# A long-convolution transform split 32 by 32 instead of 128 by 8, on small tiles of the matrix array

## The chip, the cores and the metric

The kernel runs on one core of one Trainium2 chip. The metric is the device time of one execution in microseconds (us). The engines are PE (TensorE, matmul; its weight loads are listed as PEld), DVE (VectorE), ACT (ScalarE), POOL (GpSimd) and SP (SyncE, which here only issues DMAs). SBUF is the on-chip memory in 128 partitions, PSUM the accumulator memory of PE, in 8 banks of 512 fp32 numbers per partition.

## The reference, cut to what matters

Two kinds of layer alternate on one sequence of S = 2048 tokens with D = 512 channels: a long-convolution mixer A and a channel MLP B, each with a residual and a layer norm in front.

```python
def _A_ref(q, k, v, shift_k, ssm_k, ssm_D):
    k_shift = <causal FIR of 4 taps per channel on k>
    kv = k_shift * v
    y = irfft2(rfft2(pad(kv)) * rfft2(pad(ssm_k)))[:S]     # causal convolution of length S
    y = y + kv * ssm_D
    return q * y
def _B_ref(x, w1, b1, w2, b2):                             # F = 1376
    h = gelu(layernorm(x) @ w1 + b1)
    return h @ w2 + b2
x = A_q
for _ in range(2):
    x = x + _A_ref(layernorm(x), A_k, A_v, ...)
    x = x + _B_ref(layernorm(x), B_x, B_w1, ...)
```

The convolution result y depends on k, v and the filter only, not on x. So it is computed once and used by both layers.

## The kernel before, in words

The sequence is cut into two halves of 1024 tokens. The convolution is done through a transform of length 2048 in bf16, per half: data half 0 with filter half 0 gives the output of half 0; half 1 needs data half 1 with filter half 0 plus data half 0 with filter half 1. The helper functions carry tags, which the text uses:

- `turn` (tags ht0, ht1): PE transposes bring the filter from channels-on-partitions to time-on-partitions (line 536).
- `shift_turn` and `shift`, `shift_pair` (kt, fir): the FIR of 4 taps as matmuls with diagonal weights, in half 0 on 64-row tiles of the array (line 610), in half 1 on 32-row tiles (line 638); DVE multiplies with v (lines 616, 647).
- `stage1` (h1, x1): first step of the transform, 128 matmuls per call in 8 groups, each 128 rows by 64 columns of the array, 128 columns streamed (line 553).
- `stage2` (h2, x2): second step with twiddles in a table `R_S2` of 128 x 16384 bf16 (4 MB, 16 loads of 256 KB): 128 matmuls per call in 8 groups, full array, 64 columns streamed (line 565).
- `swap`: 8 DMAs SBUF to SBUF that exchange even and odd partitions of the filter's spectrum.
- products on DVE (`tt`, line 464), `inverse1` (i1; 128 matmuls per half, line 665) and `inverse2` (i2; 16 matmuls of 512 columns per half, line 683).

Every group ends with an evacuation from PSUM by ACT or DVE (`evac`, lines 469 and 470), of 128 x 1024 numbers in most.

The MLP follows in blocks of 128 or 256 tokens for half 0 and of 512 for half 1: norms (DVE, POOL, ACT), a DMA transpose by SP (line 866; a PE transpose for the first two, line 874), `m1` with w1 (line 886, 44 matmuls a block), gelu on ACT (line 891), `m2` with w2 (line 920, 11 matmuls per 128 tokens), the residual on DVE (line 924) and stores. The last 128 tokens are done in three pieces (lines 909, 913).

What sets the order: the program first records all operations; `SEQ` is a list, fixed in the source, of all operation numbers in the order of issue, `ENGS` says which engine takes each operation that may go to several, and `BANKS` gives each PSUM tile its bank. `arrange` splits SEQ into one in-order queue per engine, and `sync` puts semaphore waits where one queue needs another. DMAs are issued by SP in their place of SEQ, a few by ACT. The convolution of half 1 stands in SEQ between the MLP operations of half 0. A "matmul" in the source is two instructions of PE: a weight load and a multiplication.

## Time and profile before

| | |
|---|---|
| median of 3 runs | 238.55 us (238.39 to 239.25) |
| span of the profiled execution | 238.6 us, from the first to the last instruction (no other time of that execution is given) |
| PE busy | 226.9 us in 2615 matmuls; weight loads 152.3 us |
| DVE, ACT, POOL busy | 178.1, 159.6, 55.3 us |
| first matmul of the MLP (line 886) | 60.40 us after the span's start |
| last DVE operation (line 913) | begins at 236.23 us |
| DMA | 26.75 MB, of it 0.34 MB in 21 packets of the queue named "instruction" |

How to read it: "busy" of PE counts pipelined matmuls, so it is not work at full speed. The time line lists instructions in order of time, merged, with the idle time before them in brackets and who ended it; "issue" there means that the engine waited for nothing that the profile shows. The chain of waits is followed back from the last instruction. A row of windows gives the busy time of each engine in a stretch with the number of its instructions, the granted clock of PE, the mean busy share of the 16 DMA engines and their rate.

### The profile page before, as it was taken

Reading aid. Unit: us, or ns where it says so; the run is one execution under the profiler, and the core shown is the slowest. Engines: PE = TensorE matmul, PEld = TensorE weight load, DVE = VectorE, ACT = ScalarE, POOL = GpSimd, SP = SyncE. Lnnn points to the kernel's source line nnn. Section 1 sums busy time; section 2 is a strip of 40 time slices with the busy share of each in tenths; the row PEclk is TensorE's granted clock in tenths of the full one; section 3 lists DMA queues with packets and bytes.
Section 4 is the critical chain, followed back from the end, with each engine's and each line's share of the span. In section 5 each row is a group of like instructions: output and inputs, shape, how many; then the busy total and the mean of one; then the engine's idle time right before and its main releaser. Section 6 shows DMA issues by size and latency. Waiting matters only on the chain.

```text
span 238.6 us, 6251 instructions
## 1 busy us (share of the span) xinstructions
PE 226.9 (95%) x2615; PEld 152.3 (64%) x2637; DVE 178.1 (75%) x358; ACT 159.6 (67%) x255; POOL 55.3 (23%) x120
## 2 busy tenths in 40 slices
PE   6998698899999999999999999999999999999995
PEld 3897588885968588667769675644445444444454
DVE  0579869999999999999999999593579469404013
ACT  2586879999996899999768786359036606831630
POOL 2421030104623506446004522303020210200000
PEclk9999979999999999999999999999999999999999
DMA  6999767989946660053100304200300050132202
GB/s 173 350 393 388 272 181 186 257 267 194 163 87 197 153 140 3 1 69 103 54 0 15 80 0 83 49 3 12 78 0 3 18 157 0 25 66 91 84 0 91
DMA packets 41112, 26.75 MB, mean 112 GB/s; under 512 B 23702, under 2 KB 33788, under 8 KB 41084
## 3 DMA queue, kind: packets, MB, share of 16 engines
q1 hardware_dynamic: 40786, 26.20, 40.5%
q8 instruction: 21, 0.34, 0.6%
q10 hardware_dynamic: 298, 0.16, 0.3%
q14 instruction: 7, 0.06, 0.1%
HBM read 15.07 MB, written 2.10 MB: 72 GB/s over the span
## 4 chain that ended last, share of the span: by engine, by line
PE 83%; DVE 6%; DMA 4%; ACT 3%; issue 2%; POOL 1%; SPq 1%; POOLq 0%
PE ps L886 32%; PE ps L920 31%; PE ps L665 6%; PE ps L553 5%; PE ps L565 3%; ACT ar L469 3%; DMA ar<-in_A_ssm_k_dram 2%; DVE ar L464 2%; DMA ar<-ar 2%; DVE ar L616 1%; PE ps L683 1%; PE ps L909 1%; PE ps L638 1%; PE ps L610 1%; DVE ar L470 1%
## 5 line engine op out<-in xcount | busy, mean ns | idle before, releaser
L891 ACT ACTIVATE ar<-ps,sm 128x256 bf16<-128x256 f32 (+4 forms) x143 | 65.4, 525 | 41.0 <-PE ps L886 39.5
L469 ACT ACTIVATE ar<-ps 128x1024 bf16<-128x1024 f32 (+3 forms) x77 | 71.3, 1005 | 16.4 <-PE ps L553 6.4
L886 PE MATMUL ps<-ar 128*128 128x256 bf16 (+4 forms) x568 | 81.5, 297 | 0.3
L920 PE MATMUL ps<-ar 128*128 128x512 bf16 (+1 forms) x324 | 77.2, 379 | 1.1 <-issue 0.3
L886 PEld LDWEIGHTS ps<-ar 128*128 128x128 bf16 (+1 forms) x572 | 52.8, 100 | 28.1 <-ACT ar L891 0.4
L464 DVE TENSOR_TENSOR ar<-ar 128x512 bf16<-128x512 bf16 (+3 forms) x105 | 62.7, 637 | 0.9 <-ACT ar L469 0.4
L920 PEld LDWEIGHTS ps<-ar 128*128 128x128 bf16 (+1 forms) x341 | 32.4, 98 | 33.4 <-ACT ar L891 0.2
L924 DVE TENSOR_TENSOR ar<-ar,ps 128x512 bf16<-128x512 bf16 x31 | 20.7, 678 | 33.2 <-PE ps L920 33.0
L797 DVE BATCH_NORM_STATS2 sm<-ar 128x6 f32<-128x512 bf16 x64 | 42.9, 683 | 0.5
L822 ACT ACTIVATE ar<-ar,sm 128x512 bf16<-128x512 bf16 x34 | 26.4, 811 | 9.5 <-DVE sm L809 8.3
L804 POOL TENSOR_TENSOR sm<-sm 128x2 f32<-128x2 f32 (+2 forms) x26 | 23.6, 909 | 23.8 <-DVE sm L802 22.0
L802 POOL TENSOR_SCALAR sm<-sm 128x2 f32<-128x2 f32 (+2 forms) x21 | 6.4, 304 | 97.3 <-DVE sm L798 97.1
L553 PE MATMUL ps<-ar 128*64 128x128 bf16 x512 | 18.6, 227 | 3.1 <-issue 1.4
L565 PEld LDWEIGHTS ps<-ar 128*128 128x128 bf16 x512 | 18.4, 102 | 3.4 <-ACT ar L469 1.0
L565 PE MATMUL ps<-ar 128*128 128x64 bf16 x512 | 19.6, 199 | 0.5 <-ACT ar L469 0.4
L553 PEld LDWEIGHTS ps<-ar 128*64 128x64 bf16 x512 | 15.7, 114 | 6.1 <-issue 2.6
L812 POOL TENSOR_SCALAR sm<-sm 128x1 f32<-128x1 f32 x43 | 16.1, 390 | 2.0
L470 DVE CAST ar<-ps 128x1024 bf16<-128x1024 f32 x11 | 13.3, 1222 | 4.3 <-PE ps L565 2.8
L665 PE MATMUL ps<-ar 128*128 128x128 bf16 x256 | 15.0, 219 | 0.5 <-DVE ar L464 0.4
L665 PEld LDWEIGHTS ps<-ar 128*128 128x128 bf16 x256 | 14.7, 113 | 1.2 <-DVE ar L464 0.6
L823 DVE TENSOR_SCALAR ar<-ar,sm 128x512 bf16<-128x512 bf16 x30 | 11.8, 410 | 3.4 <-POOL sm L812 3.1
L470 DVE COPY ar<-ps 128x1024 bf16<-128x1024 bf16 (+1 forms) x9 | 5.5, 632 | 8.0 <-PE ps L516 5.3
(41 smaller groups left out, 94.3 us busy)
## 6 DMA issues: line engine op xcount, KB each, us to landing
ar<-tab_s SPq DMA_DIRECT2D x16, 256.0 KB, 9.0
ar<-ar SPq DMA_DIRECT2D x16, 256.0 KB, 3.7
ar<-in_A_ssm_k_dram SPq DMA_DIRECT2D x8, 256.0 KB, 6.8
ar<-in_A_q_dram SPq DMA_DIRECT2D x8, 256.0 KB, 4.7
ar<-in_A_v_dram SPq DMA_DIRECT2D x8, 256.0 KB, 6.1
out_dram<-ar SPq DMA_DIRECT2D x7, 256.0 KB, 2.5
ar<-in_B_w_dram SPq DMA_DIRECT2D x4, 344.0 KB, 4.8
ar<-in_B_w_dram SPq DMA_DIRECT2D x5, 256.0 KB, 4.0
```

What stands on the lines that cost most here:

```text
L464: return P.op(eng, lambda e: e.tensor_tensor(o, a, b, op), dur, reads=[a, b] + list(more), writes=[o])
L469: return e.activation(dst, src(), AF.Copy)
L470: return e.tensor_copy(dst, src())
L553: r = e.matmul(Q(tl, 64 * ri, 64, i * 128, [1, 128]), w, m, start=True, stop=True)
L565: r = e.matmul(Q(tl, 0, 128, i // 8 * 512 + i % 8 * 4, [32, 16], [1, 4]), w, m, start=True, stop=True)
L665: r = e.matmul(Q(tl, 0, 128, i * 128, [1, 128]), w, m, start=n == 0, stop=n == 1)
L797: P.op(DVE, lambda e, sj=sj, x=x: e.bn_stats(sj, x), 600.0, reads=[x], writes=[sj])
L804: P.op(POOL, lambda e: e.tensor_tensor(r, v, hf, ALU.pow), 420.0 + 149.0 * n, reads=[v, hf], writes=[r])
L822: return e.activation(o, x, AF.Identity, bias=u, scale=r)
L886: r = e.matmul(Q(tl, 0, rows, 0, [1, w]), a, m, start=dk == 0, stop=dk == 3)
L891: P.op(ACT, lambda e, dst=dst, tl=tl, rows=rows, bias=bias, w=w: e.activation(dst, Q(tl, 0, rows, 0, [1, w]), AF.Gelu_apprx_tanh, bias=bia ...
L920: r = e.matmul(Q(tl, 0, 128, 0, [1, 512]), ins[fc][0], ins[fc][1], start=fc == 0, stop=fc == 10)
```

## The change

The transform's two steps have 32 x 32 points instead of 128 x 8. All tensors of the convolution are laid out anew: a group of 32 partitions holds 32 blocks of time or frequency of 128 channels. The matmuls then have 32 or 64 rows of the array, or 32 or 64 columns of it, and several lie beside each other in the array.

- The table of `stage2` shrinks from 128 x 16384 to 128 x 4096 bf16 (1 MB, 4 loads).
- Matmuls per half (before, then after): turn 32, then 256 in half 0 (`turn0`, two halves of the channels, each once its own two loads are there) and 128 in half 1 (`turn1`); stage1 128 per call, then 128 on 32-row tiles with 64 columns streamed; stage2 128 per call, then 256 on tiles of 32 x 64 with 128 columns streamed; FIR 88 in half 0 and 176 in half 1, then 352 in each on tiles of 64 x 32; inverse1 128, then 256 on 64-row tiles; inverse2 16 of 512 columns, then 256 on tiles of 32 x 32 with 128 columns streamed, in PSUM tiles of 4 banks.
- The evacuations stay 8 per step of 128 x 1024 numbers. The products on DVE keep their sizes, with runs of 16 numbers instead of 64.
- The swap's 8 DMAs move 2048 contiguous numbers per partition; each needs all 8 groups of stage2 (before, each needed four of them).
- v is loaded in 4 DMAs of 32 partitions in runs of 128 numbers (256 bytes), q in 4 DMAs of 32 partitions in runs of 8 KB. Stores are 4 DMAs of 32 partitions where one of 128 stood: 32 in all for 11; some go to ACT's queue.
- 40 warm-up matmuls in 10 groups of 4 are added and stand at places in the new SEQ. The filter half 1 (ht1, h1_1) shares memory with the data of half 0 and stands later. `paced` falls away (it had no effect with its distance of 99).
- SEQ, ENGS and BANKS are new.

```diff
-    S2 = S2.transpose(0, 1, 2, 3, 5, 6, 4).reshape(128, 128 * 128)
+    S2 = S2.reshape(32, 4096)
...
-        for j in range(8):
-            tl = Tile(2)
-            ins = [(ri, i, src(8 * j + i), A(0, 128, R_F + 128 * ri, [1, 128])) for i in range(8) for ri in range(2)]
-                    r = e.matmul(Q(tl, 64 * ri, 64, i * 128, [1, 128]), w, m, start=True, stop=True)
+    def mms(tl, ins, dur):
+        def f(e):
+            for tile, p0, n, off, dims, w, m, a, z in ins:
+                r = e.matmul(Q(tile, p0, n, off, *dims), w, m, start=a, stop=z)
+            return r
+        P.op(PE, f, dur, reads=[x for y in ins for x in y[5:7]], tile=tl)
...
+    def turn0():
+        for i in range(2):
+            tt(o, o, A(64 * i, 64, R_TC + 4, [5, 4]), ALU.add, {DVE: 70.0, POOL: 200.0}, (DVE, POOL))
+            for h in (1, 0):
+                src = [(a, g, A(64 * i, 64, hraw + 1024 * g + 16 * h + a, [32, 32])) for a in range(16) for g in range(4)]
+                        r = e.transpose(QB(tl, 32 * g, 32, a * 64, [1, 64]), s, idn)
...
+    def stage1(x, G):
+        for gp in range(2):
+            for hi in range(4):
+                mms(tl, [(tl, 0, 128, 512 * g + 64 * lo, ([1, 64],), A(64 * gp + 32 * g, 32, x + 1024 * hi + lo, [8, 128]),
+                          A(64 * gp + 32 * g, 32, R_F, [1, 64]), True, True) for lo in range(8) for g in range(2)], 240.0)
...
     def stage2(G, t):
-        ins = [(i, A(0, 128, R_S2 + (16 * t + i) * 128, [1, 128]), A(0, 128, G + (16 * t + i) * 8, [1024, 8], [1, 8])) for i in range(16)]
+        mms(tl, [(tl, 64 * (d // 2), 64, 512 * (d % 2) + 4 * i, ([16, 4], [64, 8], [1, 4]),
+                  A(32 * d, 32, R_S2 + 128 * (4 * t + i) + 64 * ri, [1, 64]), A(32 * d, 32, G + 256 * (4 * t + i) + 128 * ri, [1, 128]), ri == 0, ri == 1)
+                 for i in range(4) for ri in range(2) for d in (0, 2, 1, 3)], 460.0)
...
+    def shift(half):
+        for b in range(4):
+            for a in steps:
+                for r in range(2):
+                    for g in range(4):
+                        k = A(64 * r, 64, R_KT + 1152 * g + a % 8 * 144 + (16 if a >= 0 else 15) + b, [4, 32])
+            mms(tl, ins, 900.0)
...
+    def inverse2(Z, YT, groups):
+        for n in groups:
+            tl = Tile(4)
+            mms(tl, [(tl, 32 * j, 32, 512 * g + 128 * i, ([1, 128],), A(32 * g, 32, R_T2 + 32 * (2 * (8 * j + s0 + i) + ri), [1, 32]),
+                      A(32 * g, 32, Z + 128 * (2 * (8 * j + s0 + i) + ri), [1, 128]), ri == 0, ri == 1)
+                     for i in range(n) for ri in range(2) for j in range(4) for g in range(4)], 230.0 * n)
...
+                    def store(c, n, last=False):
+                        for j in range(4):
+                            src = A(32 * j, 32, R_X[half] + c, [1, n])
+                            outs.append(dma(dr(out, 512 * (1024 * half + 8 * j) + c, [32 * 512, 32], [1, n]), src, 64 * n, reads=[src], writes=[],
+                                            eng=(SP, ACT) if half and s > 4 else SP))
```

## The prediction

> **What bounds the kernel now.** I read the page first: the span, the busy shares, the DMA queues, and the chain by engine.

> ```profile
> span 238.6 us, 6251 instructions
> PE 226.9 (95%) x2615; PEld 152.3 (64%) x2637; DVE 178.1 (75%) x358; ACT 159.6 (67%) x255; POOL 55.3 (23%) x120
> ...
> q8 instruction: 21, 0.34, 0.6%
> ...
> PE 83%; DVE 6%; DMA 4%; ACT 3%; issue 2%; POOL 1%; SPq 1%; POOLq 0%
> ```

> PE is the bound, and each matmul is a pair: as many weight loads as multiplications. The queue "instruction" moved 0.34 MB in 21 packets, 16 KB each. Next come the windows, to see where PE is full (columns: PE, PEld, DVE, ACT, POOL busy with counts, granted clock, DMA share, GB/s).

> ```profile
> 0.00:10.00 10.00, 7.81 (x63) 5.09 (x65) 1.79 (x4) 2.69 (x3) 3.28 (x14) 1.00 0.77 237
> ...
> 20.00:30.00 10.00, 7.60 (x189) 6.43 (x187) 8.97 (x17) 8.32 (x9) 1.40 (x6) 1.00 0.89 317
> 30.00:40.00 10.00, 9.31 (x229) 8.80 (x223) 7.74 (x9) 8.72 (x10) 1.94 (x5) 0.83 0.73 183
> 40.00:50.00 10.00, 8.76 (x184) 8.30 (x185) 10.00 (x17) 9.41 (x12) 1.47 (x4) 1.00 0.89 267
> 50.00:60.00 10.00, 9.08 (x161) 6.67 (x160) 9.75 (x23) 9.97 (x13) 3.20 (x9) 1.00 0.92 195
> 60.00:70.00 10.00, 9.86 (x155) 7.97 (x157) 9.93 (x21) 9.48 (x28) 4.97 (x12) 1.00 0.74 132
> ```

> From 60 us PE is full, in the front it is not. Then PE's time line of the front, for the gaps that no wait explains (start, length, engine, line, count, idle before and its releaser):

> ```profile
> 22.80 0.72 PE L536 MATMUL ps<-ar 128*128 128x128 bf16 x9 [0.23 <-issue]
> 23.35 1.10 PE L565 MATMUL ps<-ar 128*128 128x64 bf16 x32
> 24.39 0.64 PE L553 MATMUL ps<-ar 128*64 128x128 bf16 x16
> 24.96 1.11 PE L565 MATMUL ps<-ar 128*128 128x64 bf16 x32
> 26.01 0.64 PE L553 MATMUL ps<-ar 128*64 128x128 bf16 x16
> 26.93 0.64 PE L553 MATMUL ps<-ar 128*64 128x128 bf16 x16 [0.28 <-ACT ar L469]
> 27.84 0.35 PE L553 MATMUL ps<-ar 128*64 128x128 bf16 x5 [0.28 <-ACT ar L469]
> 29.62 0.97 PE L553 MATMUL ps<-ar 128*64 128x128 bf16 x27 [1.42 <-issue]
> 30.52 4.52 PE L565 MATMUL ps<-ar 128*128 128x64 bf16 x96
> 34.88 0.32 PE L536 MATMUL ps<-ar 128*128 128x128 bf16 x2
> 35.72 0.53 PE L536 MATMUL ps<-ar 128*128 128x128 bf16 x6 [0.53 <-issue]
> 36.09 1.56 PE L565 MATMUL ps<-ar 128*128 128x64 bf16 x48
> 37.49 0.68 PE L536 MATMUL ps<-ar 128*128 128x128 bf16 x8
> 38.28 1.11 PE L565 MATMUL ps<-ar 128*128 128x64 bf16 x32
> 39.32 0.64 PE L553 MATMUL ps<-ar 128*64 128x128 bf16 x16
> 40.12 0.64 PE L565 MATMUL ps<-ar 128*128 128x64 bf16 x16 [0.16 <-ACT ar L469]
> 41.12 1.53 PE L553 MATMUL ps<-ar 128*64 128x128 bf16 x48 [0.37 <-ACT ar L469]
> ```

> This is the view that decides. Three gaps are put down to "issue", and two of them lie inside a group that waits for nothing: stage1's groups have 16 matmuls, and one breaks after 5; a transpose group breaks 2 and 6. Count the matmuls between them: 9+32+16+32+16+16+5 = 126 from 22.80 to 29.62, and 27+96+2 = 125 from there to 35.72. With the weight loads and a few waits that is 256 instructions both times; in 16 KB packets, 64 bytes each. I read it so: PE's instructions come in blocks of 256, and PE stood still because the next block was not there. A block then took 6.82 and 6.10 us. The next 126 end at 41.12, after 5.40 us, with no such gap (only a wait for ACT), at the lower DMA rate of the window from 30 us.

> [...]

> **The change part by part.** Prices of PE's forms, from the chain of waits (start, length, count):

> ```profile
> 7.50 1.08 PE ps L536 x8
> 15.83 1.89 PE ps L610 x44
> 43.91 3.76 PE ps L665 x64
> 60.40 3.97 PE ps L886 x68
> 72.12 1.05 PE ps L638 x87
> 98.36 1.46 PE ps L553 x48
> 114.73 3.50 PE ps L886 x32
> 188.42 9.68 PE ps L920 x44
> 236.23 0.29 DVE ar L913
> ```

> Per matmul: 64-row FIR 43 ns, inverse1 59, 32-row FIR 12, stage1 30, m1 of 256 columns 109, m2 of 512 columns 220 (its records miss some; I take 217, for inverse2 too).

> *Array time.* Before, for both halves: stage1 512 x 30 = 15.4 us, stage2 512 x 30 (its row: 96 in 4.52 us with the pipeline's end and waits, so the stage1 price) = 15.4, inverse1 256 x 59 = 15.1, inverse2 32 x 217 = 6.9, FIR 88 x 43 + 176 x 12 = 5.9, transposes 96 at some 60 = 5.8: 64 us. After: transposes 256 + 128 + 32, stage1 512, stage2 1024, FIR 704, inverse1 512, inverse2 512: 3680 matmuls. By the 32-row FIR's 12 ns that is 44 us; by stage1's 30 ns, the nearest tile that is narrow in columns, 110 us. I take 12 ns, since the new tiles are also four or more beside each other, and keep the other end for a rival. So the array is relieved by 20 us.

> [...]

> *Instructions.* PE's matmuls go from 2615 to 4686 (3680, 47 warm-ups, 5 for the taps, 8 transposes and 946 of the MLP; both lists counted off SEQ), so some 9400 instructions. Up to the first m1 of the MLP stand 2136 matmuls, 16.7 blocks; before, the six windows to 60 us hold 1070, 8.4 blocks. That doubles what the front asks of the resource that showed the gaps.

> What does a block cost? Upper end: 6.82 and 6.10 us, mean 6.4, measured beside 317 and 183 GB/s. Above nothing: the transfer itself, 0.6% of 16 x 238.6 us over 21 packets = 1.1 us, an estimate from the queue's row. 5.40 us was enough once. I take 6.4 for the first three blocks that are waited for, beside the opening loads, and 4.4 for the rest, an estimate below 5.40 since no wait showed there, and nearer to the rows than to 1.1, because a fetch must also be asked for and noticed. A block with more array work than that costs its work.

> *Sum.* The first boundary is passed at about 7 us, when the first transposes run on the filter (the chain has them at 7.50). From there to the first m1 are 16 blocks, each with 0.9 to 3.4 us of array work at the prices above: 7 + 3 x 6.4 + 13 x 4.4 = 83.4 us, against the chain's 60.40. Then 17 blocks with the MLP of half 0 and the convolution of half 1. Counted off the order, their array work is 98.3 us in all, but six hold only 3.0, 2.9, 1.3, 3.5, 2.7 and 4.3, so the 4.4 adds 8.7: 107.0. Then the MLP of half 1, in blocks of 24 to 28 us, where the fetch is hidden: 79.4. The tail: 236.23 + 0.29 to 238.6 is 2.1 us now; the last piece's store becomes 4 DMAs, two each on SP and ACT.

> ```profile
> 43.42 3.05 SPq L449 DMA_DIRECT2D ar<-in_B_w_dram  x4
> ```

> An issue is at most 0.76 us by this row, so +0 to 0.8, taken 0.5. Together 83.4 + 107.0 + 79.4 + 2.6 = 272.4. The profiled span of 238.6 and the median of 238.55 agree, so nothing is to be shifted: 272.

> *The rest.* The table's missing 3.1 MB are 9.9 us of DMA at 317 GB/s; the chain has DMA at 4%, so I give them 0 (0 to -3), and they are why I take 4.4 rather than 6.4. v in 256-byte runs may be slower by some us; it is needed by the FIR, which now stands four blocks in, so 0 (0 to 2). The swap waits for all of stage2 and has four blocks of FIR and x1 to hide in: 0. Evacuations keep count and size; ACT takes some 40 in the front, by the window from 20 us 0.92 us each, under 83 us: 0, and 44 us with the start if the fetch cover were gone. The runs of 16 on DVE: 0 (0 to 3 in half 1, where DVE is 10.00 of 10 in one window). inverse2 in 4-bank tiles beside the MLP: each holds half of PSUM for an evacuation of 1 us, four times: 0 to 4, under the fetch waits, 0. The 40 warm-ups are 40 instruction pairs, already counted. The clock: PE idles more in the front, and the window from 30 us shows 0.83; even at half clock a block's 2 us become 4, under 4.4: 0.

> **The rivals.**
> *A, the other side: the fetch hides.* Blocks arrive in under 2.5 us, from where the front is no longer set by them (7 + 3 x 6.4 + 13 x 2.5 = 58.7). For it: the loads are 3 MB less, and no gap shows at 41.12. Against it: the two measured blocks. Then the front is ACT's 44 us and some 10 of latencies between the steps, 54; and 54 + 98.3 + 79.4 + 2.6 = 234. The gain is small, as half 1's filter moves behind the first m1.
> *B, the fetch half hides*, blocks of 2.5 to 3.8 us: at 3.0 the front is 65.2, the middle 100.4, the sum 248; at 3.8 it is 262.
> *C, worse:* small tiles cost 30 ns each, as narrow column tiles do before: 46 us more than now on PE, 285; or blocks stay at 6.4 throughout, 109.4 + 123.4 + 82.0 = 315. At 5.4 it is 293.

> **How the numbers follow.** Forecast, blocks of 3.8 to 5.4 us, 262 to 293: 0.53. B, 238 to 262: 0.17. A, 224 to 238: 0.17. C, 285 to 315: 0.13. Time 272; range 238 to 293, which holds the forecast, B and a little of C. Within 0.5% (1.2 us, about what this measurement can tell from nothing) lie 0.02, between A and B; faster 0.16, slower 0.82.

> **What would show it.** Right: gaps put down to "issue" on PE every 125 to 128 matmuls of the front; "issue" a large share of the chain instead of 2%; some 35 packets and 0.57 MB in the queue "instruction"; the first m1 near 83 us; the MLP of half 1 as before, 76 to 80 us. Wrong: no such gaps in the front, or gaps shorter than 1 us; the first m1 before 60 us; small-tile groups whose matmuls start 30 ns apart.

## The result and the profile after

The changed kernel takes 282.25 us (median of 4 runs, 280.12 to 282.65) against 238.47 us (238.26 to 239.25) before: a ratio of 1.180, 95% interval 1.173 to 1.186. The forecast was 272 us, its range 238 to 293. The profiled execution took 282.53 us, its span is 280.7 us. A second set of runs gave 281.37 us (278.65 to 283.81), ratio 1.174 [1.164, 1.184]. In three sets (this second one, the filter turned in 128 rows, the filter of half 1) one run of four lies more than 1.5% above the fastest; the ratios leave it out, and the medians of the other three, 280.09, 275.75 and 278.33 us, are the ones compared below. The two sets of the same kernel, 282.25 and 280.09, differ by 2.2 us, so differences between single experiments below are good to about 2 us, and each is given against both sets.

The page of the changed kernel, the lines that answer to those of before: span, PE, the instruction queue, the chain by engine, and from the costliest groups the convolution's (busy, mean ns, idle before and its releaser).

```profile
span 280.7 us, 10373 instructions
PE 240.8 (86%) x4686; PEld 160.5 (57%) x4686; DVE 178.5 (64%) x353; ACT 163.6 (58%) x256; POOL 52.2 (19%) x117
...
q8 instruction: 37, 0.61, 1.0%
...
PE 78%; issue 9%; DMA 6%; ACT 3%; DVE 2%; SPq 1%
...
L484 PE MATMUL ps<-ar 32*64 32x128 bf16 (+7 forms) x3264 | 65.7, 241 | 25.8 <-issue 22.2
```

PE is still the engine of the chain, but "issue" has gone from 2% to 9% of it. 22.2 us of idle time, most of the 25.8 that the convolution's matmuls have, are waits for nothing that the profile shows. The 37 packets are 16 more than before, as the 2071 more matmuls with their weight loads make 16.2 blocks.

PE's time line of the front, all rows with a gap put down to "issue" up to 48 us and two more (start, length, count, idle before):

```profile
15.76 1.22 PE L484 MATMUL ps<-ar 32*128 32x64 bf16 x47 [4.44 <-issue]
...
22.77 1.38 PE L484 MATMUL ps<-ar 32*128 32x64 bf16 x39 [3.23 <-issue]
...
29.82 2.03 PE L484 MATMUL ps<-ar 32*64 32x128 bf16 x127 [0.54 <-issue]
...
34.08 2.25 PE L484 MATMUL ps<-ar 64*32 64x256 bf16 x128 [2.23 <-issue]
...
37.53 5.84 PE L484 MATMUL ps<-ar 32*64 32x128 bf16 x255 [1.21 <-issue]
...
44.93 1.30 PE L484 MATMUL ps<-ar 64*32 64x128 bf16 x78 [1.55 <-issue]
...
62.56 1.93 PE L591 MATMUL ps<-ar 128*32 128x128 bf16 x64 [3.03 <-DMA ar<-in_A_ssm_k_dram]
...
85.89 3.57 PE L886 MATMUL ps<-ar 128*128 128x128 bf16 x32
```

The row at 29.82 holds 127 matmuls and is followed by a gap, the row at 34.08 holds 128 and is followed by a gap, the row at 37.53 holds 255, which is two blocks. So the blocks of 256 instructions are seen directly. From 15.76 to 22.77 and on to 29.82 a block takes 7.0 us; from 29.82 to 34.08 it takes 4.26, from 34.08 to 37.53 it takes 3.45, and the next two together 7.40. In the profiled executions of the experiments quiet blocks take 3.3 to 4.0 us from gap to gap, beside a DMA share of 0.02 to 0.44 in the windows that hold them. Windows tell the two kinds apart (columns as in the prediction; the last two numbers but one are granted clock and DMA share):

```profile
10.00:20.00 10.00, 5.09 (x208) 4.45 (x200) 2.61 (x3) 3.23 (x4) 2.35 (x5) 0.50 1.14 247
20.00:30.00 10.00, 6.69 (x139) 6.10 (x142) 4.92 (x6) 3.88 (x4) 0.00 (x0) 0.59 1.14 236
30.00:40.00 10.00, 6.56 (x356) 5.52 (x356) 4.62 (x7) 4.23 (x5) 1.33 (x5) 0.75 0.18 63
85.90:89.30 3.40, 3.40 (x35) 3.40 (x34) 1.88 (x8) 2.78 (x7) 2.89 (x6) 0.50 0.02 5
```

The slow blocks stand beside a DMA share of 1.14, the quick ones beside 0.18. The last row holds the first 32 m1; the text comes back to it under the clock.

Where the 42.1 us between the two spans lie: the first m1 starts at 85.89 instead of 60.40 us (+25.5). The first m1 of half 1 starts at 196.11 instead of about 154.2, so the stretch between the two takes 110.2 instead of 93.8 (+16.4). From there to the end it is 84.6 instead of 84.4 us. The rows of the time lines, of before and of after:

```profile
153.74 9.34 PE L886 MATMUL ps<-ar 128*128 128x256 bf16 x44
...
163.78 1.03 PE L886 MATMUL ps<-ar 128*96 128x512 bf16 x4
```

```profile
196.11 9.67 PE L886 MATMUL ps<-ar 128*128 128x512 bf16 x44 [0.60 <-DMA ar<-ar]
```

Before, 44 + 4 matmuls stand together where a block of half 1 has 44: the first four, 0.44 us at the 109 ns of the prediction, still belong to half 0, so half 1 begins at 154.2.

What PE did with the 42.1 us: its waits put down to "issue" are 23.0 us instead of 2.7 (+20.3), its waits for a DMA 8.4 instead of 0.9 (+7.5), its busy time 240.8 instead of 226.9 (+13.9); waits for ACT and DVE grew by 0.7. So about half of the loss is seen as waiting for instructions. The front, up to the first m1, holds most of it:

```profile
PE ps L484 <- issue: 19.5, 10, 4.4
```

19.5 us instead of 2.4, so 17.1 of its 25.5 us; waits for a DMA add 4.4 there and busy time 3.7. In the stretch from there to the first m1 of half 1 it is 3.2 of 16.4: PE is busy for 103.6 us in it instead of 92.9, and it holds more of the convolution than before (stage1 224 of 512 matmuls instead of 128 of 512, stage2 512 of 1024 instead of 192 of 512).

### The profile page after: what moved, and what is told of

It reads as the page before. It is cut to its first block, busy times and chain, and to the rows that moved or that the text cites. A ratio compares the mean times of both kernels' runs of the same rounds, so it can differ in the third digit from the quotient of the medians.

```text
span 280.7 us, 10373 instructions
## 1 busy us (share of the span) xinstructions
PE 240.8 (86%) x4686; PEld 160.5 (57%) x4686; DVE 178.5 (64%) x353; ACT 163.6 (58%) x256; POOL 52.2 (19%) x117
## 3 DMA queue, kind: packets, MB, share of 16 engines
q1 hardware_dynamic: 37858, 22.77, 36.6%
## 4 chain that ended last, share of the span: by engine, by line
PE 78%; issue 9%; DMA 6%; ACT 3%; DVE 2%; SPq 1%
PE ps L886 27%; PE ps L925 25%; PE ps L484 20%; DMA ar<-in_A_ssm_k_dram 4%; DMA ar<-ar 2%; PE ps L576 2%; ACT ar L477 2%; PE ps L591 1%; ACT ar L822 1%; PE ps L628 1%; PE ps L542 1%; PE ps L914 1%; SPq L866 1%; SPq L461 1%; DVE sm L797 1%
## 5 line engine op out<-in xcount | busy, mean ns | idle before, releaser
L477 ACT ACTIVATE ar<-ps 128x1024 bf16<-128x1024 f32 (+2 forms) x76 | 73.2, 1013 | 46.0 <-PE ps L484 38.3
L891 ACT ACTIVATE ar<-ps,sm 128x256 bf16<-128x256 f32 (+5 forms) x143 | 65.6, 525 | 47.0 <-PE ps L886 46.3
L484 PE MATMUL ps<-ar 32*64 32x128 bf16 (+7 forms) x3264 | 65.7, 241 | 25.8 <-issue 22.2
L886 PE MATMUL ps<-ar 128*128 128x256 bf16 (+5 forms) x572 | 83.3, 302 | 3.9 <-DMA ar<-ar 3.1
L484 PEld LDWEIGHTS ps<-ar 32*64 32x64 bf16 (+4 forms) x3264 | 57.0, 120 | 38.9 <-issue 27.8
L886 PEld LDWEIGHTS ps<-ar 128*128 128x128 bf16 (+1 forms) x572 | 53.6, 103 | 31.6 <-DMA ar<-ar 4.1
L472 DVE TENSOR_TENSOR ar<-ar 128x512 bf16<-128x512 bf16 (+2 forms) x104 | 63.0, 641 | 4.1 <-ACT ar L477 3.1
L656 DVE TENSOR_TENSOR ar<-ps,ar 128x1024 bf16<-128x1024 f32 x8 | 9.8, 1224 | 15.1 <-PE ps L484 14.9
L478 DVE COPY ar<-ps 128x1024 bf16<-128x1024 bf16 (+2 forms) x10 | 5.9, 591 | 19.9 <-PE ps L551 5.7
L753 DVE SCALAR_TENSOR_TENSOR ar<-ar,sm,ps 128x512 bf16<-128x512 bf16 x16 | 10.9, 741 | 1.9 <-PE ps L484 1.9
L798 DVE BATCH_NORM_AGGREGATE sm<-sm 128x2 f32<-128x6 f32 x64 | 10.2, 173 | 0.7
```

The source lines that it names most:

```text
L472: return P.op(eng, lambda e: e.tensor_tensor(o, a, b, op), dur, reads=[a, b] + list(more), writes=[o])
L477: return e.activation(dst, src(), AF.Copy)
L478: return e.tensor_copy(dst, src())
L484: r = e.matmul(Q(tile, p0, n, off, *dims), w, m, start=a, stop=z)
L886: r = e.matmul(Q(tl, 0, rows, 0, [1, w]), a, m, start=dk == 0, stop=dk == 3)
L891: P.op(ACT, lambda e, dst=dst, tl=tl, rows=rows, bias=bias, w=w: e.activation(dst, Q(tl, 0, rows, 0, [1, w]), AF.Gelu_apprx_tanh, bias=bia ...
```

## The experiments

The theory: in the front, and in part of the middle, PE waits for its own instructions, at a price per block of 256 that is higher beside loads. The rivals: a fixed price or array time per small matmul; the low granted clock; and the waits for loads.

**More instructions without array work.** Four lumps of 64 matmuls of 32 x 32 with 4 columns streamed, two blocks' worth in all, in three places.

```diff
+    def tiny(tl):
+        return [(tl, 32 * (i % 4), 32, 4 * (i // 4), ([1, 4],), A(32 * (i % 4), 32, R_ID, [1, 32]),
+                 A(32 * (i % 4), 32, R_ID, [1, 4]), True, True) for i in range(64)]
     def stage2(G, t):
-        mms(tl, [(tl, 64 * (d // 2), ...
+        mms(tl, (tiny(tl) if P.tag == "h2_0" and t % 2 else []) + [(tl, 64 * (d // 2), ...
```

In the front of the changed kernel:

> The changed kernel with four lumps of 64 tiny matmuls (32 x 32 tile, 4 columns streamed, on the identity) at the head of the groups 1, 3, 5, 7 of stage2 in h2_0; the group's own matmuls then overwrite what they wrote, so the result is the same. 512 instructions more, 2 blocks of 256, in the part of the front where blocks took 3.45 to 3.95 us. Fetch theory: first m1 and total later by 6.9 to 7.9 us (7 less if a wait behind it absorbs some), gaps put down to issue grow by as much. Rival, array time: only what the 256 matmuls cost the array, which the twin run with the same lumps in the MLP of half 1 measures, 2 to 5 us.

Behind, among the wide matmuls of the MLP of half 1, where from 196.11 us on the changed kernel has no wait of PE put down to "issue":

> The changed kernel with the same four lumps of 64 tiny matmuls at the head of the sixth m1 group of each of the four MLP blocks of half 1, overwritten by the group itself, so the result is the same. There a block of 256 instructions holds 24 to 28 us of array work. Fetch theory: no gap put down to issue; the total grows by the array time of the lumps alone, 2 to 5 us (256 x 8 to 16 ns and eight changes of tile shape). Rival, a fixed price per matmul wherever it stands: the same growth as with the lumps in the front.

And in the front of the kernel before:

> The kernel before with the same four lumps of 64 tiny matmuls at the head of groups 1, 3, 5, 7 of stage2 in h2_0, overwritten by the groups, so the result is the same. There two blocks of 256 instructions took 6.82 and 6.10 us. Fetch theory: 2 blocks more, 12 to 13 us, less what slack there is behind 41 us: total +8 to +13 us, with new gaps put down to issue. Rival, array time: 2 to 5 us.

In the front it took 288.60 us (288.49 to 289.53), +6.4 against the first set and +8.5 against the second; behind 283.79 (283.32 to 287.19), +1.5 and +3.7; in the kernel before 246.26 (245.78 to 247.99) against 238.96, +7.3, ratio 1.032 [1.027, 1.036]. Of the first the first m1 and PE's waits for "issue" (us, count, longest); of the second one lump; of the third a place of PE's time line:

```profile
94.31 3.57 PE L889 MATMUL ps<-ar 128*128 128x128 bf16 x32
```

```profile
PE ps L484 <- issue: 25.8, 15, 4.6
```

```profile
196.94 0.63 PE L891 MATMUL ps<-ar 32*32 32x4 bf16 x64
197.50 7.08 PE L893 MATMUL ps<-ar 128*128 128x512 bf16 x32
```

```profile
25.47 0.32 PE L572 MATMUL ps<-ar 128*128 128x64 bf16 x5
28.63 0.74 PE L572 MATMUL ps<-ar 128*128 128x64 bf16 x11 [2.84 <-issue]
```

The two places were measured beside each other, and the front pays 4.8 us more for the same 256 matmuls. A lump's array time is 197.50 - 196.94 = 0.56 us, 2.2 for the four, which is what the place behind pays within the error (2 to 5 were expected). With these 2.2 the front's two blocks cost some 3.5 us each, a quiet block. A fixed price per matmul would be the same in both places, so this rival falls. In the kernel before, a group of 16 breaks after 5, for 2.84 us: it has the mechanism too.

Two sizes were missed. In the front the convolution's waits for "issue" grew by 3.6 us only, from 22.2 to 25.8, and the turn's wait for the filter of half 1 from 3.0 to 4.7; the first m1 moves by 8.4 us and the span by 7.0, so 1.4 come back behind it. The kernel before lost 7.3 us where 8 to 13 were expected.

**Fewer instructions, one part undone.** The filter of half 0 is turned as that of half 1, in 128 transposes of 128 rows, one block less.

```diff
-            for h in (1, 0):
-                src = [(a, g, A(64 * i, 64, hraw + 1024 * g + 16 * h + a, [32, 32])) for a in range(16) for g in range(4)]
+        turn_half(hraw, hp, (1, 0, 2, 3))
```

> One part of the change undone: the first filter half is turned in 128 transposes over all 128 rows, as the second is, instead of 256 over 64-row halves; the first m1 stage then waits for all four loads. 256 instructions less, one block, at the place where blocks took 7.0 us. Fetch theory: one gap of the front goes, first m1 and total earlier by 3 to 6 us (7 less up to 1 for the later start, and some of it absorbed). Rival, array time or clock: 0 to 1.5 us earlier, as the array streams the same number of columns per tile position.

276.72 us (275.12 to 279.44); the 275.75 named above is -6.5 against the first set and -4.3 against the second, where 3 to 6 were expected. The profiled execution took 279.44 us; its span of 277.6 us is 3.1 below the changed kernel's, its first m1 at 83.22 is 2.7 earlier, and it has 36 packets of instructions instead of 37. In it the convolution's waits for "issue" are 16.1 us instead of 22.2, while the turns wait 8.0 us for the filter's loads instead of 5.3. So turning the first half of the filter in two channel halves is by itself a loss: starting on half of the load gains less than the block of instructions costs.

**The loads beside the fetch.** Once the first loads of v in long runs, once more loads.

```diff
+        if not half:
+            for g in range(4):
+                dma(A(0, 128, R_V[0] + 1024 * g, [1, 1024]), dr(A_v, 1024 * g, [4096, 128], [1, 1024]), 1 << 18)
+            return
```

> The four loads of v for half 0 come as 128 partitions with runs of 2 KB instead of 32 partitions with runs of 256 bytes; v then lies in another arrangement in memory, so the convolution is computed with wrongly placed v, with the same instructions and waits. Theory (a block of 256 PE instructions comes later while the loads are busy, and short runs keep them busy longer): the two blocks that begin at 15.8 and 22.8 us in the changed kernel, 7.0 us each, become 5 to 6.5 us, the first m1 comes 1 to 4 us earlier, total 278.5 to 281.5 us. Rival (a block's time does not depend on the loads): the blocks stay 7.0 us, total 282.

```diff
+    for i in range(12):
+        tload(t_s2, 4096, i % 4 * 1024, R_HI + i * 1024 if i < 8 else pos[0] + (i - 8) * 1024, 1024)
```

> 12 loads of 256 KB are added behind the loads of v, as much as the table lost; nothing reads what they bring. They keep the queues busy to about 40 us. Theory (blocks come later beside loads): the blocks between 29.8 and 41 us, 3.5 to 4.3 us each in the changed kernel, become 5 to 7, total +4 to +7 us, 286 to 289. Rival (a block's time does not depend on the loads; the first blocks are slow for another reason): blocks there stay at 3.5 to 4.3, total 282 to 283.

With long runs 278.40 us (277.54 to 279.55), -3.9 against the first set of the changed kernel and -1.7 against the second; with more loads 283.60 (282.38 to 285.75), +1.4 and +3.5. The time lines, first with long runs, then with more loads, and of the latter the window from 30 us:

```profile
15.14 1.22 PE L484 MATMUL ps<-ar 32*128 32x64 bf16 x47 [4.08 <-issue]
...
22.43 1.38 PE L484 MATMUL ps<-ar 32*128 32x64 bf16 x39 [3.50 <-issue]
...
31.60 1.74 PE L484 MATMUL ps<-ar 64*32 64x256 bf16 x128 [0.52 <-issue]
```

```profile
29.65 2.03 PE L480 MATMUL ps<-ar 32*64 32x128 bf16 x127 [0.49 <-issue]
...
35.83 2.90 PE L480 MATMUL ps<-ar 64*32 64x256 bf16 x128 [4.15 <-issue]
...
40.93 5.67 PE L480 MATMUL ps<-ar 32*64 32x128 bf16 x255 [2.20 <-issue]
```

```profile
30.00:40.00 10.00, 4.57 (x246) 3.77 (x235) 4.49 (x7) 2.85 (x3) 1.32 (x5) 0.73 1.07 344
```

The added loads stretch the two blocks beside them from 4.26 and 3.45 us to 6.18 and 5.10, and the gap in front of the second from 2.23 to 4.15: the theory at the place. The total moved less than the +4 to +7 expected; the first m1 is 1.8 us later and not 3.6, since the blocks further on ran quicker in this execution (the two that follow took 6.81 us together instead of 7.40, the two that begin at 76.58 here and at 73.55 there 7.18 instead of 8.65). By the total alone it would be unclear. The bytes per second alone do not order the blocks: those of 6.18 and 5.10 us stand beside 344 GB/s, those of 7.0 us beside 236 to 247.

With long runs the first block is no shorter, 22.43 - 15.14 = 7.29 us where 5 to 6.5 were expected; only the two blocks after it are: together 31.60 - 22.43 = 9.2 us instead of 34.08 - 22.77 = 11.3. So at this place the runs of 256 bytes cost some 2 us, not by slower blocks from the start but by loads that last longer: with long runs the DMA share is 0.81 instead of 1.14 in the window from 20 us and 0.02 instead of 0.18 in that from 30. (Part of the gain is lost again: the turn waits 5.5 us for the filter of half 1 instead of 3.0.)

**The clock.** The warm-up groups stream 512 columns instead of 128, with as many instructions.

```diff
-                r = e.matmul(Q(tl, 0, 128, 0, [1, 128]), z[:, :128], z[:, :128], start=True, stop=True)
+                r = e.matmul(Q(tl, 0, 128, 0, [1, 512]), z[:, :128], z, start=True, stop=True)
```

> The 40 warm-up matmuls of the ten groups stream 512 columns instead of 128: same number of instructions, 15360 more columns on the array, so the granted clock of the front should rise from 0.5 to 0.6 in its low windows. Theory (the front waits for instructions, the clock is low because PE stands): total 281.5 to 284 us, gaps shorter by what the groups take longer. Rival (the low granted clock makes the front slow): 3 to 8 us faster, 274 to 279.

```profile
10.00:20.00 10.00, 4.64 (x207) 3.96 (x203) 2.61 (x3) 3.48 (x4) 2.16 (x5) 0.74 1.15 249
20.00:30.00 10.00, 8.45 (x157) 6.02 (x160) 5.38 (x7) 3.88 (x4) 0.00 (x0) 0.92 1.09 229
```

The clock of these windows went from 0.50 and 0.59 to 0.74 and 0.92, the total to 281.65 us (279.42 to 282.63): -0.6 against the first set and +1.6 against the second, no change that can be told. The wider matmuls also make the groups longer, so the total alone does not settle it; the blocks do. The gaps in front of the same groups end here at 16.55, 23.02 and 29.76, so the blocks take 6.47 and 6.74 us instead of 7.01 and 7.05:

```profile
23.02 1.35 PE L484 MATMUL ps<-ar 32*128 32x64 bf16 x39 [0.46 <-issue]
```

And in the profiled execution with the lumps in the front, the same two windows, which end 1.6 us behind the start of the first lump, have the full clock:

```profile
10.00:20.00 10.00, 4.74 (x173) 4.05 (x166) 2.53 (x3) 2.96 (x3) 1.83 (x3) 1.00 1.16 242
20.00:30.00 10.00, 6.18 (x143) 5.66 (x146) 5.32 (x7) 3.88 (x4) 0.00 (x0) 1.00 1.13 235
```

Its blocks there take 7.02 and 7.30 us, with gaps of 4.64 and 3.22 us. So the clock does not set these blocks. Why it is 0.50 in one execution and 1.00 in another that has such gaps too is open. Where PE comes out of the front the low clock does cost time: the first 32 m1 take 105 ns each (85.89 to 89.25) at a clock of 0.50, where the kernel before has 56 ns (68 from 60.40 to 64.20) at 1.00. That is 1.6 us, and the wider warm-up groups left it as it was: 3.57 us for these 32 in both.

**The wait for the filter of half 1.** It gets memory of its own and earlier loads.

```diff
-    R_HRAW = (R_PP, R_GB)
+    R_HRAW = (R_PP, pos[0])
```

> The filter of half 1 gets memory of its own (8 KB per partition) and its four loads are issued behind the fourth DMA of the swap, about 4 us earlier. Reading of the trace (the 3.0 us for which PE waits for this load at 62.6 us lie on the path): that wait goes, the first m1 comes 1.5 to 3 us earlier, total 279 to 281 us. Rival (the block behind it is late as well and takes the time back): the wait turns into a gap put down to issue, total 282 to 282.5.

278.53 us (277.24 to 284.87); the 278.33 named above is -3.9 against the first set and -1.8 against the second, with 1.5 to 3 expected. The first m1 is 2.5 us earlier, but this execution is 1.2 us ahead already at a row of stage1 that stands at 48.48 in the changed kernel and at 47.30 here, and the moved loads stand behind the fourth DMA of the swap (in the changed kernel its first six are issued from 47.83 on and take 3.98 us). In its time line line 586 is the turn that had waited 3.03 us:

```profile
61.79 0.56 PE L586 MATMUL ps<-ar 128*32 128x128 bf16 x20 [0.50 <-issue]
...
67.80 1.77 PE L479 MATMUL ps<-ar 64*128 64x64 bf16 x61 [2.32 <-issue]
```

The wait is gone, 1.6 us of it came back as longer gaps (0.50 new, 2.32 in front of the next block where 1.25 stood). The other 1.4 us were on the path, as the 1.3 us gained behind 48.48 say too; the totals do not tell it more closely.

**Three edits together.**

```diff
-            for i in range(4):
-                r = e.matmul(Q(tl, 0, 128, 0, [1, 128]), z[:, :128], z[:, :128], start=True, stop=True)
-            return r
+            return e.matmul(Q(tl, 0, 128, 0, [1, 512]), z[:, :128], z, start=True, stop=True)
```

with the two edits of turn and memory above.

> Three things together: the filter of half 0 in 128 transposes of 128 rows instead of 256 of 64 rows, the filter of half 1 in memory of its own with earlier loads, and the 10 warm-up groups with one matmul of 512 columns each instead of four of 128. PE gets 158 matmuls less before the first m1, 316 instructions, 1.2 blocks of 256. Theory (the front is blocks times 3.5 to 7 us each): 4.2 to 7 us by the instructions, 2 to 3 us by the load, together 272 to 276 us. Rival (the two edits gain the same microseconds, since a wait for the filter only stands in front of a block that is late anyway): 276 to 278 us. In no case faster than the kernel before.

The changed kernel beside it:

> The changed kernel as it is, beside the two runs below, so that they have their own baseline: 280 to 283 us.

275.39 us (274.09 to 277.00), -4.7 against the second set, which ran beside it, and -6.9 against the first; ratio to the kernel before 1.155 [1.148, 1.163]. Its first m1 in the time line, and PE's waits for "issue":

```profile
79.91 3.59 PE L868 MATMUL ps<-ar 128*128 128x128 bf16 x32
```

```profile
PE ps L477 <- issue: 12.5, 10, 3.2
```

It lies in the upper part of the 272 to 276 that the theory gave. The gains of turn and memory, each by itself, would be 10.4 us together against the first set and 6.1 against the second, so the three edits gave less than the sum, by 1.4 to 3.5 us; at the error of 2 that both earn partly the same microseconds is likely, not shown. The convolution's waits for "issue" fall from 22.2 to 12.5 us, with 1.7 more at the turn, but PE's waits for ACT and DVE rise from 3.4 to 10.2: where instructions no longer come last, an evacuation does. Some 37 us above the kernel before remain.

**The price of a small matmul**, measured among the wide matmuls, where no wait put down to "issue" stands in front of a lump or in it. FORMS lists rows and columns of the tile and columns streamed; all lumps of 32 rows sit on the same 32 rows of the array.

```diff
+    FORMS = [(32, 128, 64), (32, 32, 128), (32, 128, 4), (128, 128, 4)]
...
+                    tn = lump(tl, *FORMS[blk[0] - 10]) if half and fc == 5 else []
```

> 64 more matmuls on the identity stand in each of the four MLP blocks of half 1, where instructions are there in time; their results are overwritten. All sit on one row tile of 32 rows (the fourth lump on all 128 rows): tile of 128 columns with 64 columns streamed, 32 columns with 128 streamed, 128 columns with 4 streamed, full array with 4 streamed. Start to start by the trace of the changed kernel: 25 ns for the first (stage1), 10.5 to 13 for the second (inverse2). If a matmul's price goes with the columns of its tile, the third and fourth take 20 to 30 ns each; if it goes with the columns streamed, 8 to 12 ns. Total +3.5 to +6 us by the first, +2.5 to +4 us by the second; by the 12 ns taken for all small tiles +3.1 us, with all four lumps at 0.77 us.

```profile
196.15 2.04 PE L893 MATMUL ps<-ar 32*128 32x64 bf16 x64
...
220.68 1.07 PE L893 MATMUL ps<-ar 32*32 32x128 bf16 x64
...
239.51 1.75 PE L893 MATMUL ps<-ar 32*128 32x4 bf16 x64
...
258.70 1.74 PE L893 MATMUL ps<-ar 128*128 128x4 bf16 x64
```

32, 17, 27 and 27 ns each, 6.6 us in all; the total is 286.55 us (284.99 to 287.92), +4.3 against the first set and +6.5 against the second. With 4 columns streamed a tile of 128 columns still takes 27 ns, with 128 streamed a tile of 32 columns takes 17. So on one row tile the price went with the columns of the tile more than with what is streamed. Turns with neighbours on other rows of the array went with a lower price here: stage1, the first form alternating between two row tiles, takes 25.0 ns (next section) where the lump takes 32, and inverse1, with tiles of 128 columns on two row tiles, 19.0. The tile of 32 x 32 above, at 0.56 / 64 = 9 ns, alternates between four, so how much of its distance to the 27 ns is that of the columns is not shown. One price of 12 ns for all forms is wrong: these lie between 9 and 32.

## Why the prediction was right, and where not

The sign, the mechanism of the front and the size to 10 us in 282 were right: the forecast's own case, an instruction fetch that sets the front. The 9.9 us by which 272.4 was short are 2.5 in the front, 5.8 behind it and 1.6 between span and median, and the first two are each sums of larger errors that partly cancel, so the closeness is in part luck. By its steps:

- *Blocks of 256.* Right: gaps after 127, 128 and 255 matmuls, 37 packets and 0.61 MB (some 35 and 0.57 said), "issue" 9% of the chain; with matmuls this small the gaps are up to 4.44 us.
- *The front, 83.4 us.* It was 85.89. The blocks beside the opening loads took 7.0 us (6.4 taken), the quiet ones 3.45 to 3.7 (4.4 taken). The row at 29.82 was due at 7 + 3 x 6.4 = 26.2: of the 3.6 us, 1.3 are the two blocks of 7.0; the rest lies ahead of 15.76, where the first transposes waited 2.3 us for their own load. From 29.82 on, 56.1 us for 13 blocks make 4.3 each, the 4.4 of the sum, but partly for other reasons, and this is luck: the quiet blocks are shorter, while the mean holds 3.0 us of waiting for the filter of half 1, 3.4 of waiting for ACT and DVE, and blocks that stand beside the swap and the loads at 50 to 70 us.
- *The middle.* From the first m1 to the end the sum has 107.0 + 79.4 + 2.6 = 189.0 us; it was 280.7 - 85.89 = 194.8. The step that failed is the array time, 12 ns for every small matmul. The time line of the middle (start, length, count; a form's price is the distance to the next row by its count):

```profile
116.97 1.92 PE L886 MATMUL ps<-ar 128*128 128x256 bf16 x16 [1.30 <-DMA ar<-ar]
120.07 2.36 PE L886 MATMUL ps<-ar 128*128 128x256 bf16 x20 [1.18 <-DMA ar<-ar]
122.36 1.17 PE L484 MATMUL ps<-ar 64*32 64x256 bf16 x88
123.45 0.61 PE L886 MATMUL ps<-ar 128*128 128x256 bf16 x4
...
130.89 0.77 PE L484 MATMUL ps<-ar 64*32 64x192 bf16 x50 [1.83 <-issue]
...
133.88 1.27 PE L484 MATMUL ps<-ar 32*128 32x64 bf16 x48
135.08 2.55 PE L925 MATMUL ps<-ar 128*128 128x512 bf16 x11
...
145.05 1.53 PE L484 MATMUL ps<-ar 32*64 32x128 bf16 x96
146.52 2.36 PE L886 MATMUL ps<-ar 128*128 128x256 bf16 x20
...
166.19 1.88 PE L484 MATMUL ps<-ar 64*128 64x64 bf16 x96
168.01 1.04 PE L925 MATMUL ps<-ar 128*128 128x512 bf16 x4
...
175.69 0.73 PE L484 MATMUL ps<-ar 32*32 32x128 bf16 x64
176.36 1.69 PE L925 MATMUL ps<-ar 128*128 128x512 bf16 x7
```

FIR 1.09 / 88 = 12.4 ns, stage1 25.0, stage2 15.3, inverse1 19.0, inverse2 10.5. For the middle's 352, 224, 512, 256 and 256 of them that is 25.3 us where the sum had 1600 x 12 = 19.2: +6.1. Over the whole kernel the array is relieved by some 3 us and not by 20 (512 x 25.0 + 1024 x 15.3 + 704 x 12.4 + 512 x 19.0 + 512 x 10.5 = 52, and 416 transposes at 16 to 30 ns, 9, against 64 before). Against that the fetch cost the middle less than the 8.7 us taken: the gaps put down to "issue" are 3.5 us there (1.83 above, 0.80, 0.71 and 0.18), -5.2. And three waits of an m1 for a DMA within SBUF, 1.30 + 1.18 + 0.60 = 3.1 us, were not in the sum. The clock of 0.50 behind the first m1 adds the 1.6 us above, where the sum had 0. And 79.4 + 2.6 = 82.0 us for the MLP of half 1 with the tail were 2.6 short of the 84.6 measured. Together these are +8.2 where 5.8 are looked for: the sum counts by blocks, whose borders are not the rows', and some 2.4 us stay unplaced.

- *MLP of half 1 as before.* It is, 84.6 against 84.4 us. But the 79.4 of the sum does not follow from the trace of before: less a tail of 2 to 3 us both are some 82 us, above the 76 to 80 that were named.
- *The table's 3.1 MB at 0.* As much load put back behind v cost 1.4 us against the first set and 3.5 against the second: by the rows it stretched two blocks by 3.6 us together, so the term is not nothing, though its size in the total is not settled.
- *v in short runs, 0 to 2.* 2.1 us by the rows, 1.7 to 3.9 by the totals: the upper end or a little more.
- *The clock at 0.* Right for the blocks of the front; behind them it cost 1.6 us.
- *Nothing to be shifted between span and median.* Every execution here takes 1.8 us more than its span (282.53 and 280.7; of the kernel before 238.82 and 237.0), so by the same 1.8 us the span of 238.6 stood for a time of 240.4, longer than the median, and a span of 280.7 stood for 282.5 and not for itself.
- *The load of the filter of half 1* was passed over: its move behind the first data of half 0 put a wait of 3.0 us in front of the turn, of which some 1.4 were on the path.

Rival A (the fetch hides) fell with the first gap, 4.44 us in front of the row at 15.76. Rival B needed blocks of 2.5 to 3.8 us throughout; the quiet ones are like that, and it was the loads and the other waits that made the mean 4.3. Rival C's blocks of 6.4 throughout fell as well; its 30 ns per small matmul is true of none of the five forms of the middle, though 25.0 for stage1 comes near.

What stays open: why a block takes 3.45 us at a DMA share of 0.02 (34.08 to 37.53 us; the asking and noticing that the prediction gave as a reason for its 4.4 is seen in no run), and what of the loads stretches it to 7.0, their bytes or the number of their runs; the two experiments on loads show that they do, not how. The three waits for a DMA in the middle were not taken away, and no run took back the 10.7 us by which PE is busier between the first m1 of half 0 and that of half 1. So the fetch is shown as the cause of most of the front's loss, by the lumps and by the block taken out; for the middle the account rests on rows read and summed.

## What to carry to other kernels

Count a kernel's PE instructions stage by stage and divide by 256 before splitting matmuls into smaller tiles: a stage whose 128 pairs held less array work than a block took to come (3.5 us quiet, 7 us beside a DMA share of 1.14) was set by the instructions here, and the same matmuls cost only their array time beside wide ones (2.2 us for 256). A wait of PE put down to "issue" after every 127 or 128 matmuls was the sign. Behind wide matmuls, streaming fewer columns on a tile of 128 columns saved little array time here: on one row tile 64 small matmuls took 32 ns each with 64 columns streamed and 27 with 4.
